# Adding e and he² in halves before TensorE sums them, with a new weight path, pairs of decays and a new order, in a fused RWKV and SoLU kernel

## Chip, cores and metric

The kernel runs on one core of a Trainium2 chip. The metric is the device time of one execution in microseconds (us). Executions come in a fast and a slow state; verdicts use fast runs alone. The engines are TensorE (PE), VectorE (DVE), ScalarE (ACT), GpSimd (POOL) and SyncE (SP), which issues most loads.

## The reference

Batch 4, 8 heads, 768 steps, head size 48; then a feed-forward layer from 384 to 1024 and back.

```python
for t in range(S):                                   # attention, per head
    cur = einsum('bhd,bhe->bhde', u * k_t, v_t)
    y[t] = einsum('bhd,bhde->bhe', r_t, state + cur)
    state = w_t * state + einsum('bhd,bhe->bhde', k_t, v_t)
...
h = x @ w_in                                         # x: y of all heads, 384 wide
solu = h * softmax(h)
ln = (solu - mean(solu)) / sqrt(var(solu) + 1e-6) * g_ln
out = ln @ w_out
```

## The kernel before

The work is cut into 24 units of 128 steps of one batch element. Each engine issues in order, and the order is a string of words: `lw3` is the log of the decays of unit 3, `cum3` their sums, `kp3` its scaled keys, `kt3` and `kr3` their transposes, `M3` its scores, `H3` its hidden layer, `e3` and `he3` the exponential and h·e, `hq3` the square of he, `Oa3` and `Ob3` the two parts of its output products. A letter behind the number names the engine (a, v, g). `ldw3` loads the decays of unit 3.

The parts that the change and the argument touch:

```python
def setup_gain(f, engine):                   # gw: w_out scaled by the gain, bf16
    ...
def setup_mean():
    for f in range(KF):
        pe.matmul(m_ps, lhsT=mean_w, rhs=gw[:, f, :], start=(f == 0), stop=(f == KF - 1))
...
def setup_w2(f, engine):                     # eight pieces, all on GpSimd
    engine.tensor_add(out=w2[:, f, :DM], in0=gw[:, f, :], in1=mean_sb)
...
def output(i, part):
    for f in range(part * KF // 2, (part + 1) * KF // 2):
        pe.matmul(o_ps[:, :DM + 1], lhsT=he[:, f, :], rhs=w2[:, f, :], start=(f == 0), ...)
        pe.matmul(o_ps[:, DM + 1:DM + 2], lhsT=e[:, f, :], rhs=inv_col, ...)      # sum of e
    if part == 1:
        for f in range(KF):
            pe.matmul(o_ps[:, DM + 2:], lhsT=L["hq"][:, f, :], rhs=one_col, ...)  # sum of he squared
```

Eight weight pieces `w2` must exist before a unit's output is complete.

The softmax here doesn't subtract the row's maximum and nothing guards it: scores larger than these inputs give would overflow.

## Time and profile before

| | before, the profile that the prediction read | before, run again later (fast) |
|---|---|---|
| time of the profiled run | 156.91 us, slow state | 150.98 us |
| span | 155.2 | 149.3 |
| PE busy | 140.4 us, 90% | 139.1 us, 93% |
| DVE, ACT, POOL busy | 129.4, 120.2, 123.1 | 127.3, 119.4, 122.8 |
| median of the runs | 152.06 (3 runs, 151.73 to 156.62) | 151.71 (4 runs, 150.98 to 152.16) |

"Busy" is the sum of an engine's instruction times; PE's says little about how fast its products follow each other. The kernel before was run again among the experiments, and its fast profile is what the changed kernel is compared with below. Of it (busy tenths in 40 slices of 3.7 us; PEclk is the granted clock, DMA the busy share of the transfer engines):

```profile
PE   5767899599999999999999999999999999999993
...
PEclk9999999999999999999999999999999999999999
DMA  5999999998989998999999979999999111011113
```

### The profile page before, as it was taken

To read this page: it belongs to the slowest core of one execution; us is meant where nothing else is said; L and a number is where in the kernel's file an instruction comes from. 1 tells how busy PE (TensorE), PEld (TensorE's weight loads), DVE (VectorE), ACT (ScalarE), POOL (GpSimd) and SP (SyncE) were. 2 spreads that over 40 slices of the span, in tenths; PEclk is the share of its full clock that TensorE was granted. 3 is DMA by queue.
4 is the path that set the end of the run, shared out by engine and by line. 5 is a ranking of instruction groups with operands and counts; after the bars stand their busy time and mean duration, and the time that the engine had idled before them with its cause. 6 is when DMAs were issued, how large, how long until landed. Compare 5 with 4: busy or idle time off the path is not lost.

```text
span 155.2 us, 5295 instructions
## 1 busy us (share of the span) xinstructions
PE 140.4 (90%) x2156; PEld 109.7 (71%) x2156; DVE 129.4 (83%) x231; ACT 120.2 (77%) x232; POOL 123.1 (79%) x152
## 2 busy tenths in 40 slices
PE   6877897699999899999999799939999999999993
PEld 2344584477786787888788587737888778889771
DVE  7546738899998898999976989999889999998661
ACT  4456767989898979798989698829899888895742
POOL 3375965997999799999947999977799899976800
PEclk9999999999999999999999999999999999999999
DMA  4999997989999999899796999999989311011013
GB/s 95 201 185 301 380 303 152 213 160 190 208 202 184 204 229 187 194 205 233 154 205 157 218 217 200 228 250 180 215 196 211 100 51 55 2 55 55 18 62 127
DMA packets 104970, 27.09 MB, mean 175 GB/s; under 512 B 100329, under 2 KB 104562, under 8 KB 104946
## 3 DMA queue, kind: packets, MB, share of 16 engines
q1 hardware_dynamic: 104946, 26.75, 76.4%
q8 instruction: 17, 0.28, 0.7%
q14 instruction: 7, 0.06, 0.1%
HBM read 22.03 MB, written 4.72 MB: 172 GB/s over the span
## 4 chain that ended last, share of the span: by engine, by line
PE 50%; DMA 14%; DVE 10%; SPq 8%; POOL 8%; ACT 4%; issue 3%; POOLq 0%; DVEq 0%
PE o_ps L71 18%; PE h_ps L71 13%; SPq L71 8%; DMA kr_in<-in_k_dram 8%; DMA wout_f<-in_moe_w_out_dram 6%; POOL w L71 5%; PE kr_ps L71 5%; PE cum_ps L71 3%; PE m_ps L71 3%; PE y_ps L71 3%; PE s_ps L71 3%; DVE hq L71 3%; DVE kp L71 2%; PE x_ps L71 2%; DVE he L71 1%
## 5 line engine op out<-in xcount | busy, mean ns | idle before, releaser
L71 PE MATMUL o_ps<-w,he 128*128 128x385 bf16 (+2 forms) x200 | 42.2, 315 | 0.3 <-ACT sq L71 0.3
L71 PE MATMUL h_ps<-xT,win_sb 128*128 128x128 bf16 x576 | 36.0, 219 | 0.1
L71 PEld LDWEIGHTS <-win_sb 128*128 128x128 bf16 x576 | 32.9, 98 | 0.9 <-issue 0.2
L71 PE MATMUL o_ps<-inv_col,e 128*128 128x1 bf16 x192 | 31.1, 165 | 0.0
L71 DVE TENSOR_TENSOR he<-h_ps,e 128x1024 bf16<-128x1024 f32 x24 | 29.2, 1217 | 2.2 <-ACT e L71 2.2
L71 POOL TENSOR_TENSOR hq<-he 128x1024 bf16<-128x1024 bf16 x14 | 26.5, 1895 | 3.7 <-DVE he L71 2.4
L71 ACT ACTIVATE e<-h_ps 128x1024 bf16<-128x1024 f32 x24 | 24.5, 1021 | 6.2 <-PE h_ps L71 6.1
L71 PEld LDWEIGHTS <-he 128*128 128x128 bf16 x208 | 19.7, 96 | 10.5 <-issue 0.3
L71 ACT ACTIVATE cum_ps<-cum_ps 128x772 f32<-128x772 f32 (+1 forms) x24 | 19.2, 801 | 8.8 <-PE cum_ps L71 7.6
L71 DVE TENSOR_TENSOR kp<-cum_ps,kr_in 128x768 bf16<-128x768 f32 x24 | 22.7, 948 | 0.6 <-DMA kr_in<-in_r_dram 0.5
L71 POOL TENSOR_TENSOR q<-p,u_bc 128x384 bf16<-128x384 bf16 x23 | 22.0, 962 | 0.6 <-DVE p L71 0.5
L71 POOL TENSOR_TENSOR p<-kr_in 128x384 bf16<-128x384 f32 x18 | 17.9, 1001 | 5.4 <-DMA kr_in<-in_k_dram 5.4
L71 PEld LDWEIGHTS <-kp 128*128 128x128 bf16 x272 | 17.6, 102 | 4.4 <-DVE kp L71 2.3
L71 POOL TENSOR_TENSOR dv<-vb,dg 128x384 bf16<-128x384 bf16 x22 | 18.2, 830 | 2.3 <-ACT vb L71 1.5
L71 DVE TENSOR_TENSOR m<-m_ps,uts 128x1024 bf16<-128x1024 f32 x14 | 17.0, 1223 | 3.1 <-PE m_ps L71 3.0
L71 PEld LDWEIGHTS <-e 128*128 128x128 bf16 x192 | 18.3, 96 | 0.1
L71 PE MATMUL kr_ps<-ident,kp 128*128 128x128 bf16 x192 | 15.9, 230 | 1.4 <-DVE kp L71 1.4
L71 PEld LDWEIGHTS <-kr 64*128 64x128 bf16 (+1 forms) x272 | 10.7, 98 | 4.9 <-DVE kr L71 2.2
L71 ACT ACTIVATE lw<-w_in 128x384 bf16<-128x384 f32 x23 | 11.7, 523 | 2.7 <-DMA w_in<-in_w_dram 2.7
L71 ACT COPY kr<-kr_ps 128x1024 bf16<-128x1024 bf16 x13 | 13.2, 1014 | 0.5 <-PE kr_ps L71 0.4
L71 POOL TENSOR_SCALAR_AFFINE_SELECT m<-m 128x1024 bf16<-128x1024 bf16 x10 | 11.0, 1103 | 2.5 <-ACT m L71 2.4
L71 PE MATMUL cum_ps<-lw,uti_neg 128*128 128x384 bf16 x24 | 8.3, 347 | 4.8 <-DVE kp L71 3.3
(93 smaller groups left out, 284.3 us busy)
## 6 DMA issues: line engine op xcount, KB each, us to landing
w_in<-in_w_dram SPq DMA_DIRECT2D x24, 192.0 KB, 4.2
kr_in<-in_r_dram SPq DMA_DIRECT2D x24, 192.0 KB, 3.8
kr_in<-in_k_dram SPq DMA_DIRECT2D x24, 192.0 KB, 3.8
v_in<-in_v_dram SPq DMA_DIRECT2D x24, 192.0 KB, 3.8
out_dram<-o SPq DMA_DIRECT2D x23, 192.0 KB, 3.1
win_f<-in_moe_w_in_dram SPq DMA_DIRECT2D x3, 512.0 KB, 6.1
wout_f<-in_moe_w_out_dram SPq DMA_DIRECT2D x2, 768.0 KB, 8.8
out_dram<-o SPq DMA_DIRECT2D x2, 96.0 KB, 1.6
```

The source lines that it names most:

```text
L71: made = make(*args, **kwargs)
```

## The change

Its declared intent: for some units add the halves of e or of he² on VectorE or GpSimd, so that PE sums four one-column products in place of eight. The diff does more: the weights go through GpSimd's own transfer queue and are cast there or kept in fp32, five of the eight weight pieces move to VectorE in a new form, decays of two units are loaded and logged at once, and the order is new everywhere.

```diff
+    def halves(name, of):
+        def stage(i, engine):
+            t = L[name] = wk.tile([128, KF // 2, C], BF16, tag=name, name=name, bufs=3)
+            engine.tensor_add(out=t, in0=L[of][:, :KF // 2, :], in1=L[of][:, KF // 2:, :])
...
-                pe.matmul(o_ps[:, DM + 2:], lhsT=L["hq"][:, f, :], rhs=one_col, start=False, stop=(f == KF - 1),
+            hq = L.get("hs", L["hq"])
+            n = hq.shape[1]
...
     def setup_w2(f, engine):
-        engine.tensor_add(out=w2[:, f, :DM], in0=gw[:, f, :], in1=mean_sb)
+        if "scaled" in live[f]:
+            engine.tensor_add(out=w2[:, f, :DM], in0=w2[:, f, :DM], in1=mean_sb)
+        else:
+            engine.scalar_tensor_tensor(out=w2[:, f, :DM], in0=wout_f[:, f, :].bitcast(F32), scalar=gr[:, f:f + 1], in1=mean_sb,
+                                        op0=MULT, op1=ALU.add)
...
     def load_w_out(half):
+        if half == 0:
+            after(win_sb[:1, 1, :1])
         part = slice(half * KF // 2, (half + 1) * KF // 2)
-        sp.dma_start(out=wout_f[:, part, :], in_=wout_v[:, part, :])
+        pool.dma_start(out=wout_f[:, part, :], in_=wout_v[:, part, :])
...  (w_in likewise; pairs of decays; the whole ORDER string)
-... X0 m2v dv1v ldwout0 ... p2g Y1 ... X1 xT0v xT1v dg2 H0 H1 ldw3 e0 ... lw3 ... mean mean_sb:a ... cum3 wt2g ...
+... lw3 p2g sel1 q2g cum3 m2v Y0x iwout0 ... kp3 S1 X0 X1 ... kt3 H0 p3v xT1v H1 ... meanA ... mean_sb:a wt2g wt3g H2 ... wt6v ... wt1v ... wt0v wt5v ... Oa1
```

## The prediction

> **What bounds the kernel now.** I read the engines' busy shares first, then the 40 slices, then the chain of waits, then the timeline of TensorE in the windows where the chain leaves it. The times run from 151.73 to 156.62 us, and the profiled execution took 156.91 us (span 155.2): it is in the slow state, so I have to say which of its stalls a fast run need not have.
>
> The slices of the page, each 3.9 us long:
>
> ```profile
> PE   6877897699999899999999799939999999999993
> ...
> POOL 3375965997999799999947999977799899976800
> PEclk9999999999999999999999999999999999999999
> DMA  4999997989999999899796999999989311011013
> ```
>
> TensorE (PE) is full from the eighth slice on, with two dips; the granted clock is never cut. The DMA engines are full from about 4 us to 118 us and nearly idle afterwards, while TensorE works on for another 30 us. So the transfers limit how early work can start; TensorE sets the end. A busy PE is not yet a PE at its peak, so I take its real cost from the chain of waits, where one unit of work stands as a row of back-to-back pieces (start, length, what):
>
> ```profile
> 108.58 1.36 PE h_ps L71 x24
> 109.95 0.45 PE kr_ps L71 x8
> 110.39 0.33 PE m_ps L71 x8
> 110.72 1.04 PE o_ps L71 x16
> 111.76 0.39 PE y_ps L71 x12
> 112.16 0.33 PE m_ps L71 x8
> 112.48 0.44 PE s_ps L71 x5
> 112.92 0.40 PE cum_ps L71 x6
> 113.33 0.19 PE x_ps L71 x3
> 113.52 0.73 PE o_ps L71 x8
> ```
>
> One unit is these without the second m_ps: 1.36+0.45+0.33+1.04+0.39+0.44+0.40+0.19+0.73 = 5.33 us; at the smallest values that the same pieces have elsewhere in the chain about 5.1. There are 24 units, so TensorE has about 24 x 5.1 = 122 us of products that cannot overlap. The rest of the span is what I call lag: time in which TensorE was not doing them. I counted the products started by a given time, at their steady spacing (56 ns for 128 columns, 163 for 384, 25 for one). The lag is 15 us at 20 us, 20 at 35, 22 at 80, 28 at 130 and 32 at the end. Two thirds is startup, about 8 us of it stalls after 35 us, and some 4 us the tail (scaling and storing the last unit).
>
> The startup has two gates. The first hidden-layer product runs at 20 us and the first output product at 31 us; between them stands the weight w_out (chain of waits and timeline):
>
> ```profile
> 13.97 9.87 DMA wout_f<-in_moe_w_out_dram
> ...
> 26.75 7.75 POOL w L71 x8
> ```
>
> Eight additions on GpSimd, one after the other, are the last thing before the output products. The stalls after 35 us are mostly one: VectorE's square of he, normally short, took six times as long and held TensorE up. The views are that tile's and TensorE's timeline:
>
> ```profile
> L71 DVE TENSOR_TENSOR hq<-he x5: 680/692/4091, 40.9 to 148.2; 128x1024 bf16<-128x1024 bf16 x5
> ```
>
> ```profile
> 103.26 0.34 PE L71 MATMUL cum_ps<-lw,uti_neg 128*128 128x384 bf16 x1 [2.71 <-DVE kp L71]
> ```
>
> The long one ran from 98.25 to 102.34 us. With the wait of 0.60+0.47 us near 86 us and what surrounds both, such stalls make up the 4 to 5 us between this run and the fast ones, where I take it that they are absent: a fast run has about 4 us of stalls left after 35 us.
>
> **What the Trainium skill says.** "TensorE: Matmul & The Clock Gate", section "Wait — 56ns, not 53.3ns?", says that starts of products never come closer than about 25 ns however few columns they have. The trace agrees, and it contradicts what the group list suggests (165 ns each):
>
> ```profile
> 46.38 0.34 PE L71 MATMUL o_ps<-one_col,hq 128*128 128x1 bf16 x8
> 46.58 0.32 PE L71 MATMUL cum_ps<-lw,uti_neg 128*128 128x384 bf16 x1
> ```
>
> Eight one-column products occupy 46.58 - 46.38 = 0.20 us until the next product starts: 25 ns each. "SBUF — State Buffer", section "Who interferes with whom", says that a VectorE instruction with two SBUF inputs contends with a GpSimd instruction that reads SBUF, as an exclusive lock. The row above agrees: 692 ns mostly, 4091 ns once, with GpSimd products running back to back beside it. "DMA: Bandwidth & Descriptors", section "Issuing engines are not separate DMA queues", says that moving transfers to another issuing engine saves issue time only. The full DMA row fits that; that GpSimd transfers do the same no run here shows yet.
>
> **The change, part by part.**
> *Halves.* Seven units get e added in halves and five get he squared: 12 x 4 = 48 one-column products fewer, with their weight loads. At 25.5 ns that is 1.2 us, not the 48 x 165 ns = 7.9 us of the group list. Eight of the twelve are in units 18 to 22 and two in 15 and 16, where TensorE is full, so at most 40 x 25.5 ns = 1.0 us reaches the end. Price: six half-size additions on VectorE (half of 692 ns, 0.37 us each, 2.2 us) and six on GpSimd (half of 1895 ns, 0.95 us, 5.7 us).
> *Bonus through TensorE.* Eleven units instead of five add their bonus by a 384-column product: 6 x 163 ns = +1.0 us on TensorE. It moves six y copies from VectorE (549 ns) to ScalarE (474 ns). So TensorE's sum moves by only -1.2 + 1.0 = -0.2 us.
> *Log of two units at once.* 24 instructions of 523 ns become 4 of 523 and 10 of about 820 ns (384 more elements at 0.78 ns, the slope from 523 ns at 384 and 1021 at 1024): 12.5 to 10.3 us on ScalarE, and ten issues of some 0.7 us fewer in the load queue. The bytes and the 192-byte packets stay.
> *Weights.* w_in is cast on the way in: three ScalarE casts of 1046 ns go. w_out stays in fp32, its mean comes from fp32r products with a broadcast gain (+1 us once on ScalarE), and the eight GpSimd additions of 1.0 us in a row become three on GpSimd and five on VectorE, with the mean no longer waiting for all eight scaled tiles. Both leave the load queue, where one issue stood for 3.96 us behind them.
> *The new order.* Netting all counts at the group list's means: ScalarE -3.1 -2.2 -0.6 +1.0 +2.8 (y) +2.1 (two squares) -3.1 (three m) +1.0 (xT) +1.7 (three o) +0.3 = about 0; VectorE +3.7 (three m) -3.3 (y) -1.8 (o) -2.4 (p) +2.6 (w2) +2.2 (halves) -0.8 = about 0; GpSimd -3.8 (two squares) +5.7 -3.3 (three masks) +3 (p) -5 (w2) -2.5 (gains) -3 (the centring) +0.5 = about -8 us, plus issuing five transfers. So no engine that counts has less to do: the gain must come from the startup and from fewer stalls.
>
> At startup the new order does three hidden layers and the attention of four units before the first output product, some 14 us of TensorE work (four times 5.1 less 1.7 for the outputs, 13.6, plus one cum and the mean at 0.4 and 1.3, less one hidden layer of 1.34), where the old one had done 11 us by 30.9 us. I place that first output product at 31.5 to 34.5 us: w_out issued near 18 us, landed by 25 to 27, mean at 28, three w2 pieces on each engine after it. The lag there would be 17.5 to 20.5 us against 20 now: a gain of 2.5 to -0.5 us, say 1.5. With 8 us less on GpSimd the lock bites less often, and I grant 1 to 1.5 us of the remaining 4 us of stalls. Sum: 152.06 - 0.2 - 0.3 (halves land where it is full, bonus partly early) - 1.5 - 1.3 = 148.8; I set 148.6, since several changes on an already tuned schedule are more likely kept for a gain than not. That last shift is judgement, not measurement.
>
> **The rivals.**
> *Loads of unit 3 gate the start.* The new order puts cum of unit 3 and the transposes of unit 3 ahead of the first hidden layer. If w_in and w_out, now on their own queue, take turns with the loads, w and r of unit 3 come as late as 24 to 26 us and the first hidden layer moves from 20 to 26 us. For it: the full DMA row. Against: the packets are the same, and less work is left for later. It would cost all of the startup gain and up to 3 us: 151 to 153 us.
> *The lock becomes the wait.* VectorE gets twelve more instructions with two SBUF inputs (six halves, five w2, one q) and gives up three p, beside GpSimd; each may stretch as hq did. VectorE is 9.8 us of 10 busy between 130 and 140 us, so one such stretch of 3 us there goes to the end: 150 to 153 us.
> *The order is simply better.* If the lag at 35 us falls to 17 and stalls nearly vanish (0.2+0.3+3+2.5): 146 us.
>
> **Range and chances.** Good case 146, neutral 151, bad 153. The uncertainty is the schedule, not the arithmetic, so eight in ten lie in 145.5 to 152.5. The 2% borders are 149.0 and 155.1. Just over half of the weight lies under 149.0: faster 0.53, same 0.41, slower 0.06.
>
> **What would show it.** Right: 48 one-column products fewer with TensorE's busy time almost unmoved; the first output product before 34 us; a startup with more products done by 35 us than the 15 us of now; no VectorE instruction of several microseconds. Wrong: the first hidden layer waiting for unit 3; long half-additions on VectorE; a GpSimd that waits for its own transfers; fp32r products several times the 163 ns of a bf16 one; or a time below 145, which would mean that stalls in fast runs were larger than I inferred from a slow one.

## The result, and the profile after

The changed kernel took 156.56 us (median of 4 runs, 156.04 to 156.88), the kernel before, run beside it, 152.52 (4 runs, 151.73 to 156.62). A ratio in this document is the mean time of one kernel's fast runs over that of the other's fast runs of the same rounds, so it is not quite the ratio of the medians: 1.0279, 95% interval 1.0212 to 1.0346. That is **slower** by 2.8%, or some 4.3 us.

The slices of the changed kernel (3.9 us each):

```profile
PE   6977479886999999999999999999999999899991
...
PEclk9999999999999999999999999999999999999999
DMA  3999999899999899999996989897989112002032
```

TensorE is full only from the eleventh slice on, 39 us, where the fast run of before is from 30 us. I count lag as the prediction does, time minus the products started by then at their steady spacing:

| lag in us at | 20 us | 35 | 50 | 95 | 140 |
|---|---|---|---|---|---|
| before, fast profile (150.98 us) | 15.3 | 19.2 | 20.0 | 21.1 | 22.3 |
| changed (156.33 us) | 16.0 | 21.3 | 23.4 | 24.7 | 26.9 |

The sum of products went from 122.7 to 122.4 us. So of 4.6 us more lag at 140 us, 3.4 are there by 50 us; from 95 to 140 us the changed kernel gathers 2.2 us where the one before gathers 1.2.

TensorE's timeline (start, length, what; in brackets its idle time just before and what ended it) shows where the start waits. Changed:

```profile
20.28 0.48 PE L72 MATMUL cum_ps<-lw,uti_neg 128*128 128x384 bf16 x1 [2.38 <-ACT lw L72]
...
24.46 0.72 PE L72 MATMUL h_ps<-xT,win_sb 128*128 128x128 bf16 x10
...
35.31 0.34 PE L72 MATMUL o_ps<-w,he 128*128 128x385 bf16 x1 [1.11 <-DVE w L72]
```

Before, fast:

```profile
20.47 0.75 PE L71 MATMUL h_ps<-xT,win_sb 128*128 128x128 bf16 x6
...
30.27 0.32 PE L71 MATMUL o_ps<-w,he 128*128 128x385 bf16 x1
```

The first hidden layer comes 4 us later, behind the sums of unit 3, and the first output product 5 us later, after a wait for a weight piece on VectorE. The view of that tile (shortest, median, longest ns; first and last start in us) for the changed kernel:

```profile
L72 DVE SCALAR_TENSOR_TENSOR w<-wout_f,gr,mean_sb x5: 613/1181/1352, 31.8 to 37.9; 128x384 bf16<-128x384 f32 x5
...
L72 POOL TENSOR_TENSOR w<-w,mean_sb x3: 845/1137/1143, 31.8 to 33.7; 128x384 bf16<-128x384 bf16 x3
```

The one VectorE piece that runs later, beside none of GpSimd's pieces or products (only a cast overlaps it, for 0.2 us), takes 0.61 us. The other four start at 31.75 us, run beside GpSimd's three pieces and its product of r and k, and take 1.18 to 1.35 us each, 4.78 us together. The half-additions, in the same view of the changed kernel:

```profile
L72 POOL TENSOR_TENSOR es<-e x4: 1153/1157/1522, 45.0 to 142.9; 128x512 bf16<-128x512 bf16 x4
L72 DVE TENSOR_TENSOR es<-e x3: 478/1145/1332, 127.6 to 139.4; 128x512 bf16<-128x512 bf16 x3
...
L72 DVE TENSOR_TENSOR hs<-hq x3: 414/479/803, 54.4 to 144.5; 128x512 bf16<-128x512 bf16 x3
L72 POOL TENSOR_TENSOR hs<-hq x2: 1150/1152/1153, 116.6 to 140.5; 128x512 bf16<-128x512 bf16 x2
```

### The profile page after: what moved, and what is told of

Read it like the earlier page. It is cut to its first block, busy times and chain, and to the rows that moved or that the text cites.

```text
span 154.6 us, 5198 instructions
## 1 busy us (share of the span) xinstructions
PE 140.8 (91%) x2114; PEld 110.1 (71%) x2114; DVE 129.6 (84%) x230; ACT 120.5 (78%) x231; POOL 121.0 (78%) x146
## 3 DMA queue, kind: packets, MB, share of 16 engines
q1 hardware_dynamic: 103298, 23.61, 71.2%
q0 software_dynamic: 1488, 2.36, 6.6%
## 4 chain that ended last, share of the span: by engine, by line
PE 72%; DVE 7%; SPq 7%; DMA 5%; ACT 4%; issue 2%
PE o_ps L72 24%; PE h_ps L72 19%; SPq L72 6%; PE y_ps L72 6%; PE kr_ps L72 6%; PE cum_ps L72 5%; DMA w_in<-in_w_dram 5%; PE m_ps L72 4%; PE s_ps L72 4%; PE x_ps L72 3%; DVE w L72 2%; DVE m L72 2%; DVE kp L72 1%; PE mean_ps L72 1%; PE w_ps L72 1%
## 5 line engine op out<-in xcount | busy, mean ns | idle before, releaser
L72 PE MATMUL o_ps<-w,he 128*128 128x385 bf16 (+2 forms) x200 | 40.5, 316 | 1.4 <-DVE w L72 1.1
L72 DVE TENSOR_TENSOR he<-h_ps,e 128x1024 bf16<-128x1024 f32 x24 | 29.3, 1220 | 4.4 <-ACT e L72 4.2
L72 POOL TENSOR_TENSOR p<-kr_in 128x384 bf16<-128x384 f32 x22 | 22.9, 1043 | 5.2 <-DMA kr_in<-in_r_dram 5.2
L72 PEld LDWEIGHTS <-he 128*128 128x128 bf16 x208 | 18.5, 97 | 10.3 <-DVE w L72 1.3
L72 ACT ACTIVATE cum_ps<-cum_ps 128x772 f32<-128x772 f32 (+1 forms) x24 | 19.2, 801 | 7.9 <-PE cum_ps L72 6.4
L72 POOL TENSOR_TENSOR hq<-he 128x1024 bf16<-128x1024 bf16 x12 | 22.7, 1892 | 1.1 <-DVE he L72 0.8
L72 DVE TENSOR_TENSOR m<-m_ps,uts 128x1024 bf16<-128x1024 f32 x17 | 20.7, 1219 | 2.9 <-PE m_ps L72 2.7
L72 POOL TENSOR_TENSOR q<-p,u_bc 128x384 bf16<-128x384 bf16 x22 | 20.6, 942 | 0.2
L72 PE MATMUL o_ps<-inv_col,e 128*128 128x1 bf16 x136 | 14.9, 165 | 0.0
L72 ACT ACTIVATE lw<-w_in 128x768 bf16<-128x768 f32 (+1 forms) x13 | 9.9, 767 | 4.0 <-DMA w_in<-in_w_dram 4.0
L72 PE MATMUL m_ps<-kr 64*128 64x128 bf16 x192 | 10.2, 229 | 2.9 <-DVE kr L72 1.6
L72 ACT ACTIVATE o<-o_ps,rs 128x384 f32<-128x384 f32 (+1 forms) x20 | 11.5, 574 | 0.3
```

What stands on the lines that cost most here:

```text
L72: made = make(*args, **kwargs)
```

## The experiments

All 18 kernels gave correct results. In the expectations, theory S says that the start is the loss and the halves are neutral; the letters G, K and L are explained there (L is the half-additions in the first group of runs and the shared bandwidth of the loads in the second).

### The start or the halves? (four runs)

**Before again.** The kernel before, unchanged.

> The unchanged kernel once more, for a profile in the fast state and the noise of the comparison. Ratio 0.99 to 1.01. All theories: a fast profile near 151 us span, with the first output product at about 31 us, and about 4 us less of stalls after 35 us than the slow profile (which had 8). If its lag at 35 us is 20 us as in the slow profile and it grows by only 3 to 4 us to 145 us, then the change lost about 1 us by 35 us and the rest later; if the fast profile starts earlier, the startup is the larger part.

It took 151.71 us, ratio 0.9984 (0.9922 to 1.0047), and gave the fast profile used above.

**The changed kernel without halves.**

```diff
- ... es3g ... hs4v ... es16g ... hs15g ... es18v ... (all twelve words)
+ ... Oe3 Ob3 ...   (the other four sums of e, for the seven units that had es)
```

> The changed kernel with all twelve half-additions taken out (48 one-column products come back, everything else and the order stay). Theory S (startup and schedule cost the time, the halves are nearly neutral): 155 to 157.5 us. Rival L (the half-additions on VectorE and GpSimd, which stretch each other, cost it): 152.5 to 154.5 us.

It took 156.41 us (155.55 to 157.34), ratio 1.0300 (1.0224 to 1.0376), against 1.0279 with halves. To within about 1%, the halves neither cause the loss nor give a gain.

**The kernel before with the same halves.** The twelve additions are put right behind their he or hq, in place, since there is no room for new tiles.

```diff
- ... he18 ...
+ ... he18 es18v ...           (and so on; he squared likewise behind hq)
```

> The kernel before with the same twelve half-additions alone (done in place in e and in the square, as there is no room for new tiles), nothing else changed. Theory S: 151 to 153.5 us, as 1.0 us of products at the end is bought with about 9 us of VectorE and GpSimd. Rival L: over 154 us.

It took 160.11 us (159.14 to 162.1), ratio 1.0489 (1.04 to 1.0578): far more than I expected, and by the ranges a point for rival L in that order. The profiled run is a slow-state one, so its lines only illustrate. GpSimd's timeline near the end, where he's square, two half-additions and another square follow one another, and the VectorE line that waited for them:

```profile
140.23 2.07 POOL L72 TENSOR_TENSOR hq<-he 128x1024 bf16<-128x1024 bf16 x1 [0.45 <-DVE he L72]
142.38 1.15 POOL L72 TENSOR_TENSOR hq<-hq 128x512 bf16<-128x512 bf16 x1
143.49 1.15 POOL L72 TENSOR_TENSOR e<-e 128x512 bf16<-128x512 bf16 x1
144.59 1.89 POOL L72 TENSOR_TENSOR hq<-he 128x1024 bf16<-128x1024 bf16 x1
```

```profile
146.52 0.42 DVE L72 TENSOR_TENSOR hq<-hq 128x512 bf16<-128x512 bf16 x1 [3.39 <-POOL hq L72]
```

VectorE stands 3.39 us in its order for a square that GpSimd delivers late, and he of the next unit stands behind it. So the cost of a half-addition is a matter of place: nearly nothing in an order made for it, 8 us in all in one that isn't. The halves' neutrality in the changed kernel is a property of that order.

**Unit 3 moved behind the first hidden layer.**

```diff
- lw3 p2g sel1 q2g cum3 ... exp3 ... et3 ... kp3 ... kt3 H0 p3v xT1v H1 kr3a
+ p2g sel1 q2g ... H0 lw3 cum3 xT1v H1 exp3 et3 e0 kp3 p3v kt3 kr3a
```

> The changed kernel with unit 3's log, cumulative sum, decay, scaling and transposes moved behind the first two hidden layers in the order. If the wait for unit 3's w (2.4 us of TensorE at 20 us) gates the start: first hidden layer at 21 to 22 us in place of 24.5, first output product 0.5 to 2 us earlier, time 154 to 155.5 us. If w_out and the eight pieces of w2 after it are the gate: first output product still at 35 us and 156 to 157 us.

The expectation says behind both; in the kernel unit 3's log and sums stand between the two. It took 159.67 us (159.38 to 160.13), ratio 1.0516, outside both ranges. The first hidden layer came earlier (21.92 us), but the second stood:

```profile
26.63 2.42 PE L72 MATMUL h_ps<-xT,win_sb 128*128 128x128 bf16 x24 [2.01 <-DVE kp L72]
```

The sums of unit 3 and the hidden layers share two PSUM buffers, and one is free again only after unit 3's scaled keys. The attempt says that this place is bad, not whether unit 3 gates the start.

### Late weights, shared bandwidth or the lock? (four runs)

**Output weights issued earlier.**

```diff
-        if half == 0:
-            after(win_sb[:1, 1, :1])
...
- iwin2 kt2 ... Y0x iwout0 ldv2 dv1v exp3 iwout1 Y1x
+ iwin2 iwout0 iwout1 kt2 ... Y0x ldv2 dv1v exp3 Y1x
```

> The changed kernel with one thing moved: the two loads of the output weights are issued as soon as GpSimd's third load of input weights is issued (about 14.7 us instead of 19 and 20), and no longer wait until those have landed. Theory G (the late output weights start the loss: landed 28.9 us against 21.6 before, and everything to the first output product hangs on them): they land at 24 to 26 us, the mean products end by 28, the first output product comes at 31.5 to 33.5 us instead of 35.3, and the time is 153 to 155 us. Rival K (the lock [...]between VectorE and GpSimd is what delays the first output product): the weights land early but the first output product stays at 34.5 to 36 us, 155.5 to 157.5 us. Rival L (all loads share one bandwidth, so what the output weights gain the input weights and keys lose): the first product of h moves from 24.5 to 26 us or later, and the time is 156 to 158.

It took 160.8 us (158.91 to 161.37), ratio 1.0544 (1.0461 to 1.0627): 4 us worse than the changed kernel. The output weights did land earlier (their last packet ended at 24.32 us instead of 28.93), but the first hidden layer moved from 24.46 to 27.38 us. Theory L holds, more strongly than I had put it. What theory G expected of this edit did not come; whether the late weights would cost time if nothing else were delayed to bring them forward, this run cannot say. This profile is a slow-state one; the fast profile of the fourth run of this group has the same early issue, and its chain of waits (start, length, what) shows the mechanism:

```profile
12.76 11.71 DMA kr_in<-in_r_dram
...
24.57 0.96 DVE kp L72
25.53 0.48 DVE st L72
...
26.05 1.01 PE kr_ps L72 x8
27.06 4.94 PE h_ps L72 x48
```

This load, r of unit 3, took 11.71 us while the weights streamed on the other queue; in the run that differs by the early issue alone (the third of this group) the same load took 7.31 us, and its kind takes a median of 4.6 in the changed kernel; the hidden layers stood behind unit 3's keys.

**VectorE's five pieces in one row** (the control of the next run).

```diff
- wt2g wt3g H2 ... wt6v y3a wt1v ... wt0v wt5v X3 ... Oa1 wt7v
+ wt2g wt3g wt1v wt0v wt5v wt6v wt7v H2 ... y3a ... X3 ... Oa1
```

> The changed kernel with VectorE's five scaled-weight pieces put in its order directly one behind the other, and nothing else; it is the control of the next run. The pieces keep their two SBUF inputs. Theory K (the lock): they still take 1.1 to 1.4 us each beside GpSimd's three, the first output product comes at 34.5 to 36 us and the time is 155.5 to 157.5. If the order alone was what held them, the first output product comes at 33.5 us or earlier and the time is 153.5 to 155.5.

It took 159.77 us (159.09 to 161.13), ratio 1.0531. The pieces stayed long, as theory K has it, but the time was worse than either number. Five long ones in a row keep VectorE for 6 us, and unit 4's scaled keys, which free a PSUM buffer, come late. VectorE's and TensorE's timelines:

```profile
31.87 5.97 DVE L72 SCALAR_TENSOR_TENSOR w<-wout_f,gr,mean_sb 128x384 bf16<-128x384 f32 x5 [0.36 <-ACT mean_sb L72]
```

```profile
39.29 0.50 PE L72 MATMUL cum_ps<-lw,uti_neg 128*128 128x384 bf16 x1 [3.10 <-DVE kp L72]
```

**The same, with the mean read from PSUM.** VectorE's pieces then have one SBUF tensor as input in place of two.

```diff
-        copy(engine, g_wide, gr.unsqueeze(2).to_broadcast([128, KF, 128]))
+        act.mul(out=g_wide, in_=gr.unsqueeze(2).to_broadcast([128, KF, 128]), mul=-1.0 / DF)
...
-            act.mul(out=mean_sb, in_=live[0]["mean_ps"], mul=-1.0 / DF)
+            act.copy(out=mean_sb, in_=live[0]["mean_ps"])
...
-            engine.scalar_tensor_tensor(..., in1=mean_sb,
+            engine.scalar_tensor_tensor(..., in1=live[0]["mean_ps"],
```

> As the run before it, but VectorE's five pieces read the mean from PSUM where the products left it (the factor of the mean is put into the wide gamma), so that each has one SBUF input in place of two; GpSimd's three still read the copy in SBUF. Theory K (the lock): the pieces fall from about 1.2 to 0.5 to 0.7 us, GpSimd's to 0.9 or less, the first output product comes at 32.5 to 34 us, and the time is 154 to 155.5 us. Theory G alone (only the late weights matter): the pieces get shorter but the time stays within 0.7 us of the run before it. If it is no lock, the pieces stay above 1 us.

It took 154.35 us (153.34 to 155.53), ratio 1.0164 (1.0096 to 1.0232): 5.4 us less than its control, with nothing else changed. The pieces fell to 0.61 us on VectorE and 0.83 on GpSimd, and the first output product came at 33.06 us. This is the lock: that the mean is read from PSUM is not by itself what makes a piece short, since in the changed kernel the piece beside none of GpSimd's took 0.61 us with both tensors in SBUF.

**Early output weights and pieces from PSUM together.**

> The early issue of the output weights and the pieces from PSUM together. If G and K are both links of the same chain and add up: first output product at 29.5 to 31.5 us (before: 30.3), time 151.5 to 153.5 us, so level with the kernel before to within 1 %. If something else in the new order holds the start (the late first product of h at 24.5 us, the order of the other units), the first output product comes at 32 us or later and the time stays at 154.5 us or more.

It took 158.56 us (157.56 to 160.74), ratio 1.0416. The early issue costs 4 us here as well; the gates do not add up, because issuing early was never a gain.

### What of the loss is the lock, and what is the rest? (four runs)

**The mean from PSUM in the changed kernel's own order.** The same edit as above, without the moved words.

> The changed kernel in its own order, with VectorE's five scaled-weight pieces reading the mean from PSUM; nothing is moved. Theory K (the lock makes the pieces long, and that is most of the loss): the pieces take 0.6 us, the first output product comes at 32.5 to 34.3 us, and the time is 153.5 to 155 us, as in the run with the moved pieces. Rival (the gain of that run came from moving the pieces together with the shorter pieces, or PSUM being held longer by the mean costs it back): 155.5 us or more.

It took 153.68 us (153.19 to 154.4), ratio 1.0128 (1.0085 to 1.0172). The tile's view:

```profile
L72 DVE SCALAR_TENSOR_TENSOR w<-wout_f,gr,mean_ps x5: 608/611/616, 31.8 to 35.9; 128x384 bf16<-128x384 f32 x5
...
L72 POOL TENSOR_TENSOR w<-w,mean_sb x3: 827/830/845, 31.8 to 33.4; 128x384 bf16<-128x384 bf16 x3
```

From 1.0279 to 1.0128 is 1.5%, 2.3 us of the 4.3 by these ratios: about half of the loss is the lock on the weight pieces (by the two intervals 0.7 to 2.3%, or 1 to 3.5 us). VectorE's four first pieces, started at 31.80 us as before, held it for 2.19 us instead of 4.78; the first output product came at 34.09 us instead of 35.31, and the lag at 50 us fell from 23.4 to 21.5.

**Pieces from PSUM in a row, without halves.**

> The run with the pieces from PSUM (154.35 us), without the twelve half-additions. It asks where the 2.4 us are that still lie between that run and the kernel before; 1.7 us of it is lag gathered between 95 and 140 us, where eight of the halves are and where one of them on VectorE was seen to take 1.15 us and to hold up he and the scores' products by 0.56 us. If the halves' waits are worth more than the 1.2 us of products that they save: 152.5 to 153.7 us. If they cancel, as in the changed kernel without halves: 153.8 to 155 us. If they gain now that the start is mended: 155 to 156 us.

It took 153.65 us (151.89 to 154.44), ratio 1.0099 (1.004 to 1.0157). The median lies at the edge of the first range, but the interval overlaps that of the run with halves (1.0164), so "they cancel" is what can be said. (The 1.7 us of the expectation is too much: counted as above, the run with halves gathers 2.3 us there and the kernel before 1.2.) The halves do cause waits. VectorE's and TensorE's timelines of the run with halves and the mean from PSUM:

```profile
129.04 1.15 DVE L72 TENSOR_TENSOR es<-e 128x512 bf16<-128x512 bf16 x1
130.11 1.21 DVE L72 TENSOR_TENSOR he<-h_ps,e 128x1024 bf16<-128x1024 f32 x1
```

```profile
131.37 0.40 PE L72 MATMUL m_ps<-kr 64*128 64x128 bf16 x8 [0.44 <-DVE he L72]
```

The half-addition takes 1.15 us beside GpSimd, he starts late behind it, and TensorE waits 0.44 us. Over the fast profiles the lag from 95 to 140 us grows by 2.2 us in the changed kernel and by 2.2 or 2.3 in four variants of it that keep the halves, and by 1.3 in the changed kernel without them. That is some 0.9 us of waits, 0.7 of them on TensorE's own list of waits, against the 40 products of 25.5 ns, 1.0 us, that are saved between there and the end.

**Pieces from PSUM, with decays loaded and logged one unit at a time.**

```diff
- ldw4 ... lw4 ...        (a pair each)
+ ldw4 ldw5 ... lw4 lw5 ...
```

> The run with the pieces from PSUM, with the log decays of each unit loaded and taken alone, as before the change (ten loads and ten logs more). If the pairs help as predicted (2.2 us of ScalarE, some 7 us of issuing): 155 to 157 us. If they don't matter, within 0.7 us of 154.35. If the pairs cost (a load of 384 kB holds up the keys behind it at the start): 152 to 153.6 us, with the lag at 50 us lower than 20.5.

It took 154.0 us (152.95 to 155.18), ratio 1.0162: the pairs do not matter by any amount that these intervals show (about 0.9%). They spare ScalarE its 2 us and the load queue ten issues, but not its time: SyncE's issues of loads add up to 91.9 us with pairs and 92.6 without, since the issues that remain take longer.

**The kernel before, two weight pieces from PSUM.**

```diff
- cum3 wt2g y2v exp3 lw4 et3 p3v hq0a wt3g cum4 wt1g X2 dm0 wt0g ... S2 kt3 ... Oa0 kp4
+ cum3 wt2g wt1v wt0v y2v exp3 lw4 et3 hq0a wt3g cum4 p3g X2 dm0 ... S2 Oa0 kt3 ... kp4
-    in1=mean_sb
+    in1=live[0]["mean_ps"] if engine is dve else mean_sb
```

> A candidate to beat both: the kernel before, in which two of GpSimd's eight weight pieces (1 and 0) go to VectorE and read the mean from PSUM, unit 3's product r times k goes from VectorE to GpSimd, and the first four output products of unit 0 are put ahead of the transposes of unit 3. If the chain of eight GpSimd additions is what the start hangs on: the first output product comes at 28.5 to 29.5 us instead of 30.3, and the time is 150.3 to 151.3 us against 151.7. If the loads of units 4 and 5 hold the start anyway: within 0.5 us of the kernel before.

It took 151.58 us (6 runs, 151.05 to 152.69), ratio 1.0010 (0.9973 to 1.0047). The first output product did come 1.6 us earlier, at 28.63 us, and the lag at 30 us was 18.1 instead of 19.0, but at 35 us it was 19.2 in both. TensorE's timeline of this run has the waits that took the gain:

```profile
27.44 0.32 PE L71 MATMUL cum_ps<-lw,uti_neg 128*128 128x384 bf16 x1 [1.31 <-ACT lw L71]
...
31.10 0.40 PE L71 MATMUL m_ps<-kr 64*128 64x128 bf16 x8 [0.70 <-DVE p L71]
```

The first of them is in the kernel before too, with the same 1.31 us; the second is new. The eight GpSimd additions were not by themselves what held the start.

### Unit 3 and the rest (six runs)

**Unit 3's decays ahead of its keys in the load queue**, on the run with moved pieces from PSUM.

```diff
- ldv1 q0v kt1 ldk3 cum2 ... kp2 ldw3 vb1a
+ ldv1 q0v kt1 ldw3 cum2 ... kp2 ldk3 vb1a
```

> The run with the moved pieces from PSUM (154.35 us; lag 19.4 us at 35 us and 20.5 at 50), with one exchange in the load queue: unit 3's decays are loaded where its keys were, and its keys where its decays were, two places later. If unit 3's decays gate the start: TensorE's wait for the log of unit 3 (2.1 us) falls under 1 us, the first hidden-layer product comes at 22 to 22.5 us instead of 23.5, and the time is 152.8 to 153.6. If the time saved there is only waited for elsewhere: within 0.6 us of 154.35.

It took 153.1 us (151.75 to 153.16), ratio 1.0075 (0.9995 to 1.0156), 1.2 us under its base. TensorE's wait for the log of unit 3 is gone, and the first hidden layer came at 22.48 us instead of 23.49. But the first output product moved only from 33.06 to 32.79 us and the lag at 50 us from 20.5 to 20.2, so the trace accounts for 0.3 us; the intervals of the two ratios overlap. Unit 3's decays may be a part of the rest, of 0.3 us by the trace and 1.2 at most by the medians.

**Unit 3's chain behind the second hidden layer**, on the same base (he of unit 1 moves with it).

```diff
- lw3 ... cum3 ... exp3 ... et3 ... kp3 ... kt3 H0 p3v xT1v H1 kr3a e0 ... he0 Y2x y2a gw2a S2 q3g M3
+ ... H0 xT1v H1 e0 ... he0 lw3 Y2x y2a gw2a S2 cum3 he1 exp3 et3 kp3 p3v kt3 kr3a q3g M3
```

> The same base, with unit 3's log, sums, exponents, scaled keys and transposes moved behind the second hidden layer, where the kernel before has them, and the loads left as they are. If unit 3 gates the start: first hidden-layer product at 20.5 to 21.5 us, no wait for PSUM buffers in the second one, lag at 35 us 18.5 or less, time 152 to 153.4 us. If the scaled keys of unit 3, now late, hold up its scores instead: first hidden layer early, but lag at 50 us 20.5 or more and 154 to 156 us.

It took 160.03 us (158.56 to 164.36), ratio 1.0528, worse than either range. The first hidden layer came at 22.08 us, and then TensorE's timeline reads:

```profile
30.08 0.62 PE L72 MATMUL kr_ps<-ident,kp 128*128 128x128 bf16 x8 [2.10 <-DVE kp L72]
31.80 0.61 PE L72 MATMUL m_ps<-kr 64*128 64x128 bf16 x8 [1.11 <-ACT kr L72]
...
32.71 1.84 PE L72 MATMUL mean_ps<-wout_f,g_wide 128*128 128x384 f32 x4
```

The products of the mean, at 28.02 us in the base, stand behind unit 3's scores in TensorE's order and start 4.7 us later. Here unit 3 early is a price that the rest of the order needs.

**Both edits, and both without halves.**

> Both edits. If unit 3 gates the start, no better than the better of the two (the wait that the exchange shortens is no longer ahead of anything): 152 to 153.4 us. If it doesn't: 154 to 156.

> Both edits and no half-additions: the halves cancelled in two pairs of runs, so within 0.8 us of the run with both edits, whichever way that goes. Under 151.5 us it would beat the kernel before; I don't expect it.

They took 159.73 us (159.6 to 160.32, ratio 1.0548) and 159.44 us (159.12 to 160.07, ratio 1.0527), the first of them outside both of its ranges. The late chain decides both, and the halves are neutral for a third time; the lag from 95 to 140 us grew by 2.3 us with and 1.4 without them.

**The repairs together**, in the changed kernel's own order: mean from PSUM, unit 3's decays first, no halves.

> The changed kernel in its own order, with the mean read from PSUM, unit 3's decays loaded before its keys, and no half-additions. Alone, the mean from PSUM gave 153.7 us and the load order 1.2 us on top of the other variant; halves were neutral within 0.7. If the three are the whole loss: 151.5 to 152.8 us, ratio 1.000 to 1.010. If a further cost of the new order remains: 153 to 154 us.

It took 153.13 us (152.26 to 155.29), ratio 1.0084 (1.0036 to 1.0131): by the ratio inside the first range, by the time inside the second, so a further cost of the new order remains. The two edits added to the lock's repair give nothing that can be told from zero (1.0128 before them), and 0.4 to 1.3% stay.

**The kernel before, with three moves:** the two pieces from PSUM, the sums of unit 4 behind the state products of unit 2, and unit 4's scaled keys ahead of the state copy.

```diff
- cum4 p3g X2 ... exp4 lw5 ... kp3 S2 Oa0 kt3 ldv3 cum5 st2 ... et4 kr3a xT2v ... kp4
+ p3g X2 ... kp3 S2 cum4 exp4 Oa0 lw5 ... kt3 ldv3 et4 kp4 cum5 st2 ... kr3a xT2v
```

> The kernel before with two weight pieces from PSUM, and with unit 4's sums put behind the state products of unit 2, unit 4's scaled keys ahead of the state copy. If TensorE's wait of 1.3 us for the log of unit 4 can be filled with other work: 150.2 to 151 us against 151.2 to 151.7 of the kernel before. If the scores of unit 3 and the loads of unit 5 hold it anyway: 151.2 to 152 us.

It took 152.01 us (6 runs, 151.49 to 152.74), ratio 1.0030 (0.9995 to 1.0065). No version beat the kernel before.

**The clock is not the cause.** Most profiles of the changed variants show TensorE's granted clock cut for a part of the first 50 us, and most of their timed runs have a mean clock of some 0.95. The kernel before has such a mean in about half of its fast runs, without a price: the mean of 24 fast runs with a clock above 0.99 is 151.60 us, that of 21 with 0.95 to 0.97 is 151.72. The changed kernel's one run at 0.998 took 156.33 us, inside the range of the others.

## Why the prediction was wrong

The prediction said 148.6 us, between 145.5 and 152.5, most likely faster; it was 156.56 and slower.

**What bounds the kernel** held in its frame: TensorE's products can't overlap and make 122 us, and the time is decided by lag. The 4 us of stalls that it gave a fast run after 35 us, worked out from a slow one, were 3.1 by 140 us. It was wrong in one reading. "Eight additions on GpSimd, one after the other, are the last thing before the output products" holds for four of them: the eight run to 34.50 us, and the first output product is at 30.92. Nor is that row what the start hangs on: with the first output product 1.6 us earlier (28.63 us) the kernel before took the same time. The last wait in a chain is not what the chain is worth; other waits stand just behind it.

**Halves.** The 48 products fewer are there, and the products' sum moved by about -0.2 us, as predicted. The price was put too low: GpSimd's six additions took 7.3 us instead of 5.7 (1.15 us each, not 0.95), VectorE's six 4.7 instead of 2.2 (up to 1.33 us each, not 0.37). "At most 1.0 us reaches the end" became nothing that three pairs of runs show, and waits of some 0.9 us in the same stretch fit that.

**Bonus and logs.** Eleven bonus products as counted; a pair of logs took 841 ns, near the 820. Loading and logging in pairs was not worth any time that shows.

**Weights.** This is the step that failed: "The lag there would be 17.5 to 20.5 us against 20 now: a gain". It was 21.3 at 35 us, and 19.2 in a fast run of before: the 1.5 us of gain in the sum was a loss of 2.1, and of 3.4 by 50 us. The first output product was set at 31.5 to 34.5 us and came at 35.31. Of its terms, w_out was issued at 18.96 us (I said near 18), landed at 28.93 (25 to 27), the mean's products began at 29.0 (28), and "three w2 pieces on each engine after it" was priced as if they ran side by side. They hinder one another: 1.18 and 1.14 us in place of 0.61 and 0.83. Taking that away gave back 2.3 us (1 to 3.5) in the order as it is, and put the first output product at 34.09 us, inside the range. The fp32r products, which the prediction feared, follow each other 0.17 us apart and are no part of it.

**The new order.** GpSimd was to lose about 8 us, "plus issuing five transfers". Its busy time fell by 1.8 us, which counts that issuing: it stands in GpSimd's own order for 3.5 us. The halves cost 1.6 us more than predicted, and smaller items the rest. The "1 to 1.5 us of the remaining 4 us of stalls" that were to go did not go: from 35 to 140 us the changed kernel gathers 5.6 us of lag, the fast kernel before 3.1.

**The rivals.** "The lock becomes the wait" was the right mechanism. I put it in the stretch from 130 to 140 us and at 150 to 153 us, although the five weight pieces were in its list; they were its main place, some 100 us earlier. "Loads of unit 3 gate the start" was seen in the trace (the first hidden layer at 24.46 us, after 2.38 us for the log of unit 3), but taken away by an exchange in the load queue it was worth 0.3 us by the trace and 1.2 by the medians, whose intervals overlap. Its premise that transfers on the other queue slow the loads was shown by the runs with early output weights.

**What stays open** is the last part of the loss, 0.8% with all three repairs (interval 0.4 to 1.3%), about 1.3 us. That it lies in the start of the new order is suggested by lags at 50 us of 20.2 to 21.5 us in its variants against 20.0, but no run isolates it. One candidate was never tested by itself: w_out lands some 7 us later than in the kernel before (29.3 against 22.2 us, by the semaphores of the second half), and the only edit that brought it forward delayed other loads.

**On the Trainium skill.** "SBUF — State Buffer", section "Who interferes with whom", which the prediction quoted for one stretched square, states both the cause and the cure: a VectorE instruction with at most one SBUF input, outside the two-port modes, does not contend with GpSimd. The pair of runs (159.77 and 154.35 us, pieces of 1.2 and 0.61) agrees. "DMA: Bandwidth & Descriptors", section "Queues, rings and completion order", says that each transfer engine takes turns between the queues it has work for, a whole packet at a time. That fits a load that went from 7.31 to 11.71 us: by the profile of the changed kernel, GpSimd's queue moved 2.36 MB in 1488 packets, 1.6 kB each, and the load queue 23.61 MB in 103298, 229 bytes each. That the size of the packets is the reason was not tested.

## What to carry to other kernels

Before two engines are given equal shares of one small job, look at where their operands lie: with two SBUF inputs on VectorE and a neighbour on GpSimd, the split pays for itself only in part, and one operand left in PSUM removes the conflict. A load issued earlier on a second queue is not free, because it takes from the loads already under way. And the last wait of a chain must be removed in a run before it is counted as a gain, with the next wait behind it named.

## What the Trainium skill lacked or had wrong

- "SBUF — State Buffer", section "Who interferes with whom": it calls the shared ports an exclusive lock, under which the one who comes second blocks for the whole instruction, and gives no size for short instructions that take turns. Here pieces of 0.61 us (VectorE) and 0.83 us (GpSimd) became 1.18 and 1.14 us, each less than the sum of 1.44, so the two overlap in part. Its list of operations names `tensor_tensor` for this; here the form with a scalar and two SBUF tensors does the same.
- "DMA: Bandwidth & Descriptors", section "Issuing engines are not separate DMA queues": it says that a second issuing engine only saves issue time. It has no number for the cost: with 1.5 MB of weights issued 4 us earlier on GpSimd's queue, a load on SyncE's queue took 11.71 us instead of 7.31, and the kernel 4 us more.
- "DMA: Bandwidth & Descriptors" has no number for the time that GpSimd's own order loses to issuing: 0.63 us for each transfer of w_in and 0.78 for each of w_out.
- No page that I read gives the time of a short GpSimd addition. Half the elements cost more than half here: an addition of 128x512 in bf16 took 1.15 us, where the square of 128x1024 took 1.89.
